# Sliding-window attention with ALiBi, then a hard-swish MoE layer: another PSUM bank plan for the end of batch 0

## The chip, the core and the metric
The kernel runs on one core of a Trainium2 chip. The metric is device time in microseconds (us), lower is better. The core's engines have queues of their own that run side by side and meet only at semaphores: TensorE (PE: matmuls, transposes as matmuls with an identity, and its weight loads, PEld), VectorE (DVE), ScalarE (ACT), GpSimd (POOL, which here also issues DMAs), and SyncE (SP, which only issues DMAs). Matmul results land in PSUM, which has eight banks[...].

## What is computed
For 8 batches of 8 heads, 576 positions and head size 64, attention looks back at most 127 positions and has a bias that falls with the distance; its output, 4608 tokens of 512 values, goes through two dense layers with a hard-swish between them.

```python
scores = scale * np.matmul(q, k.transpose(0, 1, 3, 2))
bias = slopes[:, None, None] * (-np.abs(rel).astype(np.float32))[None, :, :]
mask = (rel >= 0) & (rel < window)          # window = 128
scores = np.where(mask, scores + bias[None], -1000000000.0)
attn = softmax over the last axis
x = (attn @ v).transpose(0, 2, 1, 3).reshape(B * S, H * D)
h = x @ w_in                                # 512 -> 2048
out = (h * np.clip(h + 3.0, 0.0, 6.0) / 6.0) @ w_out
```

## The kernel before
**Pairs.** Attention is worked in 32 steps g, one for each pair of heads of a batch (NP = 4 pairs a batch: g 0 to 3 are batch 0, 4 to 7 batch 1). The steps of a pair are functions, each of which puts its instructions at the end of every engine's queue; the order is written out by hand (`tc.manual_schedule`), so the order of the calls is the order of each queue.

- `transposes(g)` (L218): 24 PE transposes of 96x64 make q and k column-wise, into two PSUM tiles `tp`. `settle(g)` (L237) copies them to SBUF (`qTb`, `kTb`).
- `scores(g)` (L248): matmuls into two double-bank tiles, `scd` (blocks on the diagonal) and `sco` (blocks beside it). For g up to 8 the bias comes in by a matmul with a table (L257, L260).
- `exp_diag`, `exp_off` (L285, L300): ACT takes exps of them to SBUF (`pd`, `po`, `p4buf`), POOL masks `po` (L306). In `first_batch` the three calls of a pair are `exps(g)`.
- `values(g, qts)` (L321): matmuls with v for query blocks 0 to 2 (tile `av`) and 3 to 4 (tile `avh`), each followed on DVE by the norm: a reciprocal (L343) and a multiplication into `avs` (L344). `both(g)` is the two calls.
- `back(g)` (L353): for batches 0 to 2, five PE transposes of `avs` into a tile `tb` (L364), and a copy of it into `xT` (L366), the input of the dense layers.

**Dense layers.** `moe_up` (L372) is a unit of four matmuls into a tile `hps` (L377), a relu on ACT (`r`, L381) and a product on DVE (`g`, L382) that frees the bank. `moe_down` (L385) is four matmuls of the second layer (L409). `fill(n)` (L429) puts the next n units into the queues. A unit of `moe_up` over 512 tokens needs all four pairs of their batch in `xT`.

**PSUM.** Four pools share the eight banks: `ps_sc` (two tiles of two banks, for scores), `ps_av` (one bank), `ps_h` (two banks) and `ps_o` (one bank). A tile waits until the last reader of the one that had its place before is done. In batches 0 and 1 `ps_h` holds `tp` and `hps`, `avh` is in `ps_h` for g below 3 and else in `ps_o`, and `tb` is in `ps_o`.

**Order.** `first_batch` (L504) runs pairs 0 to 3 up to their exps, with the transposes of the next pair in between; the values of pairs 0 to 3, their transposes back and pairs 4 and 5 of batch 1 follow in one stretch (the drain, L531 to L553). Then `segment` (L558) goes from g = 5 on: scores(g), transposes and settle of g+1, exps(g), values(g-1), back(g-1), with `fill` calls in between, whose numbers for g = 5 to 8 are in `FILLS` (L555). Loads stand in `stage_next(g)` (L443): POOL issues those of q and k of batches 0 to 2 (L101) and the weights (L169, L174), SP those of v and of later batches (L120). Values v are cast to bf16 by `cast_v` (L178). `more_constants` (L162) makes the eight biases `bias_d`, used from g = 9 on, and a memset of `tbuf`.

```python
        scores(3); exps(3); prepare(5); both(0); turn(4); both(1); stage_next(3)
        scores(4); exps(4); prepare(6); back(0); both(2); back(1)
        turn(5); both(3); back(2); stage_next(4)
        for j in range(3):
            cast_v(1, j, nc.gpsimd)
        scores(5); back(3)
```
(The drain, with its calls run together; `turn(g)` is transposes(g) and settle(g).)

Of the kernel before, what the change touches and what calls it, by code (L numbers as in the profile page):

```python
# [11 lines left out]
BF16 = mybir.dt.bfloat16  # L12
# [6 lines left out]
def kernel(  # L19
# [9 lines left out]
    nc = tc.nc  # L29
# [6 lines left out]
    NP = H // 2  # L36
# [4 lines left out]
    RP, RT = 96, 6  # L41
# [31 lines left out]
    ps_h = ctx.enter_context(tc.tile_pool(name="ps_h", bufs=2, space=bass.MemoryType.PSUM))  # L73
    ps_o = ctx.enter_context(tc.tile_pool(name="ps_o", bufs=1, space=bass.MemoryType.PSUM))
# [87 lines left out]
    def more_constants():  # L162
        for h in range(H):
            nc.vector.tensor_scalar(out=bias_d[:, h:h + 1], in0=rel_f, scalar1=-64.0,
                                    scalar2=slopes[h], op0=ALU.add, op1=ALU.mult)
        nc.gpsimd.memset(tbuf[64:128, :, 4, :], 0.0)
# [11 lines left out]
    def cast_v(b, j, eng):  # L178
        n = min(128, S - j * 128)
        copy = nc.scalar.copy if eng is nc.scalar else eng.tensor_copy  # L180
        copy(out=vbuf[b % 2][:n, j, :, 0:D], in_=ld[b, "v"][:n, j, :, :])
# [23 lines left out]
    def prepare(g):  # L205
        b, hp = divmod(g, NP)
        hs = slice(2 * hp, 2 * hp + 2)
        for nm in "qk":
# [6 lines left out]
            copy(out=pr, in_=wide[nm])  # L215
            st[g, nm] = pr

    def transposes(g):  # L218
        b, hp = divmod(g, NP)
        if g > 2 * NP:  # L220
            pair = ps_sc.tile([128, 2, 512], FP32, tag="sc", name="tpp")
        tps = {}
        for nm in "qk":
            src = st.pop((g, nm))
            if g > 2 * NP:
                tp = pair[:, "qk".index(nm), 0:S // 2].bitcast(BF16).rearrange(
                    "p (t a) -> p t a", t=RT)
            else:
                tp = ps_h.tile([128, RT, RP], BF16, tag="h", name="tp", padded_shape=[128, 8, 128])
            for t in range(RT):  # L230
                for e in range(2):
                    nc.tensor.transpose(tp[e * D:(e + 1) * D, t, :], src[:, e, ts(t, D)],
                                        ident[:RP, :RP])
            tps[nm] = tp
        st[g, "tps"] = tps

    def settle(g):  # L237
        b, hp = divmod(g, NP)
        tps = st.pop((g, "tps"))
        for nm, dst in (("q", qTb[b % 2]), ("k", kTb[b % 2])):  # L240
            eng = nc.scalar.copy if nm == "k" and g == 0 else nc.vector.tensor_copy
            eng(out=dst[:, hp, :, :].rearrange("p j c -> p (j c)")[:, 0:S].rearrange(  # L242
                "p (a t) -> p a t", t=RT), in_=tps[nm].rearrange("p t a -> p a t"))

# [76 lines left out]
    def values(g, qts):  # L321
        b, hp = divmod(g, NP)
        vb = vbuf[b % 2]
        pd, po, p4 = st[g, "pd"], st[g, "po"], p4buf[g % 4]
        if g < 2 * NP and qts[0] > 0:
            pool, tag = (ps_h, "h") if g < NP - 1 else (ps_o, "o")
            av = pool.tile([128, 3, 2, W], FP32, tag=tag, name="avh", padded_shape=[128, 3, 2, 85])
        else:
            av = ps_av.tile([128, 3, 2, W], FP32, tag="av", name="av")
        nq = len(qts)  # L330
        for i, qt in enumerate(qts):
            for e in range(2):
                h = 2 * hp + e
                if qt > 0:
                    nc.tensor.matmul(av[:, i, e, :], lhsT=po[:, e, qt - 1, :],  # L335
                                     rhs=vb[:, qt - 1, h, :], start=True, stop=False)
                d = pd[:, e, qt, :] if qt < 4 else p4[:, e, :]
                nc.tensor.matmul(av[:, i, e, :], lhsT=d, rhs=vb[:, qt, h, :],  # L338
                                 start=(qt == 0), stop=True)
        if qts[0] == 0:  # L340
            st[g, "avs"] = small.tile([128, NQ, 2, D], BF16, tag="avs", name="avs")
        rc = small.tile([128, 3, 2, 1], FP32, tag="rc", name="rc")
        nc.vector.reciprocal(rc[:, 0:nq, :, :], av[:, 0:nq, :, D:W])  # L343
        nc.vector.tensor_tensor(  # L344
            out=st[g, "avs"][:, qts[0]:qts[0] + nq, :, :], in0=av[:, 0:nq, :, 0:D],
            in1=rc[:, 0:nq, :, :].to_broadcast([128, nq, 2, D]), op=ALU.mult)
# [3 lines left out]
    def by_xbar(g):  # L350
        return XBAR_X and g >= NB_PE * NP and g % NP < NP - 1

    def back(g):  # L353
        b, hp = divmod(g, NP)
        avs = st[g, "avs"].rearrange("p j e d -> p j (e d)")
        if by_xbar(g):
            nc.sync.dma_start_transpose(
                out=xT[:, hp, ds(b * S, SP)].rearrange("p (j c) -> p j c", j=NQ),
                in_=avs.rearrange("p j c -> p (j c)"))
            return  # L360
        pool, tag = (ps_o, "o") if b < 2 else (ps_h, "h")
        tp = pool.tile([128, SP], BF16, tag=tag, name="tb", padded_shape=[128, 1024])
        for j in range(NQ):
            nc.tensor.transpose(tp[:, ts(j, 128)], avs[:, j, :], ident)  # L364
        eng = nc.scalar.copy if b == 0 and g != 2 else nc.vector.tensor_copy
        eng(out=xT[:, hp, ds(b * S, S)], in_=tp[:, 0:S])  # L366

    gts, ops = {}, {}
# [134 lines left out]

    def first_batch():  # L504
        transposes(0)
        settle(0)
        biases()
        prepare(1)
        def exps(g):
            exp_diag(g, 0)  # L510
            exp_off(g, 0)
            exp_off(g, 1)

        def both(g):
            values(g, (0, 1, 2))
            values(g, (3, 4))

        def turn(g):
            transposes(g)
            settle(g)  # L520

        for g in range(3):
            scores(g)
            exps(g)
            turn(g + 1)
            prepare(g + 2)
            for j, eng in (((0, nc.vector), (1, nc.vector)), ((2, nc.gpsimd),),
                           ((3, nc.vector), (4, nc.vector)))[g]:
                cast_v(0, j, eng)
            stage_next(g)  # L530
        more_constants()  # L531
        scores(3)
        exps(3)
        prepare(5)
        both(0)
        turn(4)
        both(1)
        stage_next(3)
        scores(4)
        exps(4)  # L540
        prepare(6)
        back(0)
        both(2)
        back(1)
        turn(5)
        both(3)
        back(2)
        stage_next(4)
        for j in range(3):
            cast_v(1, j, nc.gpsimd)  # L550
        scores(5)
        back(3)
        done[0] = NP  # L553

    FILLS = {5: (2, 0, 0, 0, 2, 2, 0), 6: (0, 0, 0, 0, 2, 2, 0),  # L555
             7: (0, 0, 0, 0, 2, 1, 0), 8: (0, 0, 0, 0, 2, 1, 0)}

    def segment(lo, hi, fills):  # L558
        for g in range(lo, hi + 1):
            f = fills(g)  # L560
            if by_xbar(g - 2):
                done[0] = g - 1
            pe_next = g + 1 < hi and (g + 1) // NP < NB_PE
            if lo < g < hi:
                scores(g)
            fill(f[0])
            if pe_next and g < 2 * NP:
                transposes(g + 1)
                settle(g + 1)
            if g == NP + 1:  # L570
                cast_v(1, 3, nc.vector)
                cast_v(1, 4, nc.vector)
            if g < hi:
                exp_diag(g, 0)
            fill(f[1])
            if g < hi:
                exp_diag(g, 1)
            if g >= lo:
                values(g - 1, (0, 1, 2))
            fill(f[2])  # L580
            if pe_next and g >= 2 * NP:
                transposes(g + 1)
            if g < hi:
                exp_off(g, 0)
            fill(f[3])
            if g < hi:
                exp_off(g, 1)
            if g >= lo:
                values(g - 1, (3, 4))
            if pe_next and g >= 2 * NP:  # L590
                settle(g + 1)
            fill(f[4])
            if g >= lo:
                back(g - 1)
                if not by_xbar(g - 1):
                    done[0] = g
            if g + 2 < hi and (g + 2) // NP < NB_PE:
                prepare(g + 2)
            fill(f[5])
            if g < hi:  # L600
                stage_next(g)
            fill(f[6])
# [3 lines left out]
    with tc.manual_schedule(engines=every):  # L606
# [11 lines left out]
        first_batch()  # L618
        segment(NP + 1, G, lambda g: FILLS.get(g, (1, 1, 1, 1, 1, 1, 2)))
        done[0] = G  # L620
# [34 lines left out]
```

## Time and profile before

| what | value |
|---|---|
| time, median of 5 runs | 342.98 us (342.53 to 345.0) |
| the profiled execution | 348.89 us, span 347.2 us |
| mean granted PE clock in it | 0.966 |
| busy: PE / DVE / ACT / POOL | 324.3 / 176.0 / 196.2 / 139.7 us |
| matmuls of the dense layers: L377 x576, L409 x560 | 150.8 us, 141.8 us |
| transposes back on ACT / DVE, first 70 us (copy xT, L366) | 638 / 450 ns |
| copies of q and k (L242) on ACT / DVE | 638 / 747 to 757 ns |
| DMA, first 80 us | 189 GB/s |

The page gives busy times of one profiled execution; the difference of 1.7 us between its time and its span lies outside the program's instructions. A row of the timeline is: start, duration (of a merged run), engine and line, operation, out<-in, and in square brackets how long the engine was idle before it and what released it. Granted clock is the share of full speed that PE was allowed.

### The profile page before, as it was taken

Reading aid. Unit: us, or ns where it says so; the run is one execution under the profiler, and the core shown is the slowest. Engines: PE = TensorE matmul, PEld = TensorE weight load, DVE = VectorE, ACT = ScalarE, POOL = GpSimd, SP = SyncE. Lnnn points to the kernel's source line nnn. Section 1 sums busy time; section 2 is a strip of 40 time slices with the busy share of each in tenths; the row PEclk is TensorE's granted clock in tenths of the full one; section 3 lists DMA queues with packets and bytes.
Section 4 is the critical chain, followed back from the end, with each engine's and each line's share of the span. In section 5 each row is a group of like instructions: output and inputs, shape, how many; then the busy total and the mean of one; then the engine's idle time right before and its main releaser. Section 6 shows DMA issues by size and latency. Waiting matters only on the chain.

```text
span 347.2 us, 7083 instructions
## 1 busy us (share of the span) xinstructions
PE 324.3 (93%) x2759; PEld 168.9 (49%) x2759; DVE 176.0 (51%) x364; ACT 196.2 (57%) x345; POOL 139.7 (40%) x246
## 2 busy tenths in 40 slices
PE   6777799899999999999999999999999999999995
PEld 5565355545444454444445545454554444444443
DVE  4664558766545554545455555545455534434410
ACT  3742457566666666666666666675766344343401
POOL 8645326736385465186456634733333000000000
PEclk9965679999999999999999999999999999999999
DMA  9999999999996899789949994520211000110021
GB/s 171 210 214 192 175 186 151 214 183 205 243 231 143 188 227 209 139 175 216 234 115 213 188 229 115 124 79 3 79 52 51 30 30 32 50 40 32 30 91 61
DMA packets 134865, 48.17 MB, mean 139 GB/s; under 512 B 121392, under 2 KB 130352, under 8 KB 134832
## 3 DMA queue, kind: packets, MB, share of 16 engines
q1 hardware_dynamic: 122464, 33.89, 53.4%
q0 software_dynamic: 8704, 7.44, 14.0%
q10 hardware_dynamic: 3664, 6.39, 5.3%
q8 instruction: 21, 0.34, 0.4%
q14 instruction: 12, 0.10, 0.1%
HBM read 36.70 MB, written 9.44 MB: 133 GB/s over the span
## 4 chain that ended last, share of the span: by engine, by line
PE 71%; ACT 7%; DVE 7%; issue 5%; DMA 4%; POOL 4%; SPq 2%; POOLq 0%; DVEq 0%
PE hps L377 31%; PE ops L409 27%; DVE g L382 3%; ACT r L381 3%; ACT po L303 2%; DMA ldbuf<-in_k_dram 2%; POOL pd L296 2%; SPq L120 2%; PE av L338 2%; PE scd L269 2%; DMA ldbuf<-in_q_dram 1%; PE sco L275 1%; PE av L335 1%; PE ops L393 1%; DVE qTb L242 1%
## 5 line engine op out<-in xcount | busy, mean ns | idle before, releaser
L382 DVE SCALAR_TENSOR_TENSOR g<-r,hps 128x512 bf16<-128x512 f32 x144 | 98.8, 687 | 137.1 <-ACT r L381 136.9
L381 ACT ACTIVATE r<-hps,bias 128x512 f32<-128x512 f32 x144 | 99.5, 691 | 112.1 <-PE hps L377 110.8
L377 PE MATMUL hps<-xT,w_in_sb 128*128 128x512 bf16 x576 | 150.8, 387 | 5.5 <-DVE g L382 5.5
L409 PE MATMUL ops<-w_out_sb,g 128*128 128x512 bf16 x560 | 141.8, 379 | 0.0
L409 PEld LDWEIGHTS <-g 128*128 128x128 bf16 x560 | 54.3, 98 | 63.6
L377 PEld LDWEIGHTS <-w_in_sb 128*128 128x128 bf16 x576 | 51.8, 99 | 60.8 <-issue 12.8
L306 POOL TENSOR_SCALAR_AFFINE_SELECT po<-po 128x512 bf16<-128x512 bf16 x62 | 39.1, 639 | 43.9 <-ACT po L303 41.1
L296 POOL TENSOR_SCALAR_AFFINE_SELECT pd<-pd 128x512 bf16<-128x512 bf16 x46 | 28.0, 632 | 46.7 <-ACT pd L293 46.5
L303 ACT ACTIVATE po<-sco,bias_o 128x512 bf16<-128x512 f32 x62 | 41.7, 687 | 0.0
L195 POOL CAST tbuf<-ldbuf 128x512 bf16<-128x512 f32 (+1 forms) x50 | 28.3, 611 | 29.9 <-issue 25.9
L344 DVE TENSOR_TENSOR avs<-av,rc 128x384 bf16<-128x384 f32 (+1 forms) x56 | 28.0, 500 | 1.9
L293 ACT ACTIVATE pd<-scd,bias_d 128x512 bf16<-128x512 f32 x46 | 28.9, 683 | 0.0
L338 PEld LDWEIGHTS <-pd 128*128 128x128 bf16 x248 | 18.9, 101 | 9.0
L335 PE MATMUL av<-vbuf,po 128*128 128x65 bf16 x220 | 21.3, 196 | 0.7 <-POOL po L306 0.7
L335 PEld LDWEIGHTS <-po 128*128 128x128 bf16 x248 | 19.4, 101 | 5.3 <-issue 1.5
L338 PE MATMUL av<-vbuf,pd 128*128 128x65 bf16 x234 | 21.7, 198 | 0.0
L415 ACT COPY osb<-ops 128x512 f32<-128x512 f32 x18 | 10.5, 586 | 12.8 <-PE ops L409 12.8
L314 ACT ACTIVATE p4buf<-sco,bias_d 128x64 bf16<-128x64 f32 x46 | 14.8, 322 | 0.0
L417 DVE COPY osb<-ops 128x512 f32<-128x512 f32 x17 | 11.6, 684 | 5.8 <-PE ops L409 5.8
L269 PE MATMUL scd<-qTb,kTb 64*128 64x128 bf16 x256 | 13.1, 225 | 0.0
L343 DVE RECIPROCAL rc<-av 128x6 f32<-128x6 f32 (+1 forms) x56 | 10.2, 182 | 3.9 <-PE av L338 3.9
L275 PE MATMUL sco<-qTb,kTb 64*128 64x128 bf16 (+1 forms) x256 | 12.2, 218 | 0.0
(85 smaller groups left out, 213.0 us busy)
## 6 DMA issues: line engine op xcount, KB each, us to landing
ldbuf<-in_v_dram SPq DMA_DIRECT2D x32, 256.0 KB, 5.6
out_dram<-osb ACTq DMA_DIRECT2D x23, 256.0 KB, 3.5
ldbuf<-in_q_dram SPq DMA_DIRECT2D x20, 256.0 KB, 5.2
ldbuf<-in_k_dram SPq DMA_DIRECT2D x20, 256.0 KB, 5.8
out_dram<-osb SPq DMA_DIRECT2D x12, 256.0 KB, 2.0
w_in_sb<-in_moe_w_in_dram POOLq DMA_DIRECT2D x4, 512.0 KB, 8.9
w_out_sb<-in_moe_w_out_dram POOLq DMA_DIRECT2D x4, 512.0 KB, 9.0
ldbuf<-in_v_dram SPq DMA_DIRECT2D x8, 128.0 KB, 6.2
```

Source lines behind the costliest of these rows:

```text
L195: nc.gpsimd.tensor_copy(out=tbuf[:m, :, j, :], in_=s[:m, j, :, :].rearrange("p (i e) d -> p i (e d)", e=2))
L293: nc.scalar.activation(out=pd[:, e, :, :].rearrange("p j c -> p (j c)"), in_=sc[:, e, :], func=ACT.Exp, bias=bias_d[:, h:h + 1], scale=scale)
L296: nc.gpsimd.affine_select(out=pd[:, e, :, :], in_=pd[:, e, :, :], pattern=[[0, 4], [1, 128]], channel_multiplier=-1, base=0, compare_op=AL ...
L303: nc.scalar.activation(out=po[:, e, :, :].rearrange("p j c -> p (j c)"), in_=sc[:, e, :], func=ACT.Exp, bias=bias_o[:, h:h + 1], scale=scale)
L306: nc.gpsimd.affine_select(out=po[:, e, :, :], in_=po[:, e, :, :], pattern=[[0, 4], [-1, 128]], channel_multiplier=1, base=-1, compare_op=A ...
L335: nc.tensor.matmul(av[:, i, e, :], lhsT=po[:, e, qt - 1, :], rhs=vb[:, qt - 1, h, :], start=True, stop=False)
L338: nc.tensor.matmul(av[:, i, e, :], lhsT=d, rhs=vb[:, qt, h, :], start=(qt == 0), stop=True)
L344: nc.vector.tensor_tensor(out=st[g, "avs"][:, qts[0]:qts[0] + nq, :, :], in0=av[:, 0:nq, :, 0:D], in1=rc[:, 0:nq, :, :].to_broadcast([128, ...
L377: nc.tensor.matmul(hps, lhsT=w_in_sb[:, ks, ts(ms, 128)], rhs=xT[:, ks, ts(nt, NT)], start=(ks == 0), stop=(ks == n_ks - 1))
L381: nc.scalar.activation(out=r6, in_=hps, func=ACT.Relu, bias=bias3[:, 0:1], scale=1.0 / 6.0)
L382: nc.vector.scalar_tensor_tensor(out=gts[nt][:, ms, :], in0=r6, scalar=1.0, in1=hps, op0=ALU.min, op1=ALU.mult)
L409: nc.tensor.matmul(ops[nt, sub], lhsT=gts[nt][:, ms, ts(sub, 128)], rhs=w_out_sb[:, ms, :], start=(ms == 0), stop=(ms == n_ms - 1))
```

## The change
The change touches batch 0 and the beginning of batch 1 only.

- Banks: `avh` is in `ps_o` except for g = 3; `tb` is in `ps_h` for g = 0, 1 and 3, and else, in batches 0 and 1, in `ps_o`; pair 5's `tp` are in a score tile (as those of g over 8 already are); k's `tp` of pairs 6 to 8 is in `ps_o`.
- Engines: ACT copies k of pair 4 and q and k of pair 5; of the copies of xT, ACT has pairs 0 and 3, DVE 1 and 2. Cast v(0,3) goes from DVE to POOL and stands a pair earlier; v(0,4) stays on DVE.
- Order: back(0) stands ahead of scores(4), back(1) right behind it, back(3) ahead of scores(5). `more_constants` goes from ahead of scores(3) to behind the casts of batch 1 in g = 5. The first two units of the dense layers in g = 5 stand apart, one ahead of pair 6's transposes, one behind them and exp_diag(5).

```diff
+    def in_sc(g):
+        return g > 2 * NP or g == NP + 1
+
     def transposes(g):
         b, hp = divmod(g, NP)
-        if g > 2 * NP:
+        if in_sc(g):
             pair = ps_sc.tile([128, 2, 512], FP32, tag="sc", name="tpp")
...
-            if g > 2 * NP:
+            if in_sc(g):
...
-                tp = ps_h.tile([128, RT, RP], BF16, tag="h", name="tp", padded_shape=[128, 8, 128])
+                pool, tag = (ps_o, "o") if nm == "k" and NP + 1 < g <= 2 * NP else (ps_h, "h")
+                tp = pool.tile([128, RT, RP], BF16, tag=tag, name="tp", padded_shape=[128, 8, 128])
...
-            eng = nc.scalar.copy if nm == "k" and g == 0 else nc.vector.tensor_copy
+            by_act = g == NP + 1 or (nm == "k" and g in (0, NP))
+            eng = nc.scalar.copy if by_act else nc.vector.tensor_copy
...
-            pool, tag = (ps_h, "h") if g < NP - 1 else (ps_o, "o")
+            pool, tag = (ps_h, "h") if g == NP - 1 else (ps_o, "o")
             av = pool.tile([128, 3, 2, W], FP32, tag=tag, name="avh", padded_shape=[128, 3, 2, 85])
...
-        pool, tag = (ps_o, "o") if b < 2 else (ps_h, "h")
+        pool, tag = (ps_h, "h") if b > 1 or g in (0, 1, 3) else (ps_o, "o")
...
-        eng = nc.scalar.copy if b == 0 and g != 2 else nc.vector.tensor_copy
+        eng = nc.scalar.copy if g in (0, 3) else nc.vector.tensor_copy
...
-            for j, eng in (((0, nc.vector), (1, nc.vector)), ((2, nc.gpsimd),),
-                           ((3, nc.vector), (4, nc.vector)))[g]:
+            for j, eng in (((0, nc.vector), (1, nc.vector)),
+                           ((2, nc.gpsimd), (3, nc.gpsimd)), ((4, nc.vector),))[g]:
                 cast_v(0, j, eng)
             stage_next(g)
-        more_constants()
         scores(3)
...
         both(1)
+        back(0)
         stage_next(3)
         scores(4)
         exps(4)
         prepare(6)
-        back(0)
+        back(1)
         both(2)
-        back(1)
         turn(5)
...
+        back(3)
         scores(5)
-        back(3)
         done[0] = NP

-    FILLS = {5: (2, 0, 0, 0, 2, 2, 0), 6: (0, 0, 0, 0, 2, 2, 0),
+    FILLS = {5: (1, 1, 0, 0, 2, 2, 0), 6: (0, 0, 0, 0, 2, 2, 0),
...
                 cast_v(1, 4, nc.vector)
+                more_constants()
```

## The prediction
> **What bounds the kernel now.** I read the slices of the page first, then TensorE's waits, then the timeline and the one-microsecond windows of the drain of batch 0.
>
> ```profile
> PE   6777799899999999999999999999999999999995
> PEclk9965679999999999999999999999999999999999
> DMA  9999999999996899789949994520211000110021
> ```
> A slice is 8.7 us. From the sixth on PE is full but for one, and from the seventh at full clock; the slack lies in the first 50 us, where PE stops and runs at half clock (slices 3 to 6). What PE waits for from 50 us to the end:
> ```profile
> PE hps L377 <- DVE g L382: 5.5, 12, 0.7
> PE av L335 <- POOL po L306: 0.7, 2, 0.3
> ```
> That is 6.2 us in 297 (1.1 in two more rows), in a pattern that repeats. So the end moves by what the start moves. My marker is the end of the sixth up-projection unit (four hps matmuls), 48.72 us (chain of waits: 46.19 + 2.53); after it the instruction order of every engine is the same in both kernels. Before it, the timeline has these PE stops:
> ```profile
> 21.02 0.69 PE L232 MATMUL tp<-ident,ldbuf 96*64 96x96 bf16 x12 [1.50 <-DMA ldbuf<-in_k_dram]
> ...
> 26.69 0.66 ACT L366 COPY xT<-tb 128x576 bf16<-128x576 bf16 x1
> 27.40 0.69 PE L364 MATMUL tb<-ident,avs 128*128 128x128 bf16 x5 [1.02 <-ACT xT L366]
> 28.82 0.76 DVE L242 COPY qTb<-tp 128x576 bf16<-128x576 bf16 x1 [1.52 <-PE tp L232]
> 29.50 0.75 DVE L242 COPY kTb<-tp 128x576 bf16<-128x576 bf16 x1
> 31.54 0.71 PE L364 MATMUL tb<-ident,avs 128*128 128x128 bf16 x5 [1.25 <-DVE avs L344]
> 39.40 0.45 PE L232 MATMUL tp<-ident,ldbuf 96*64 96x96 bf16 x12 [0.92 <-DVE g L382]
> 41.15 0.21 PE L338 MATMUL avh<-vbuf,pd 128*128 128x65 bf16 x1 [0.87 <-DVE vbuf L181]
> 41.92 0.21 PE L338 MATMUL avh<-vbuf,p4buf 128*128 128x65 bf16 x1 [0.39 <-DVE vbuf L181]
> ```
> Each number in brackets is idle PE. W0 (1.50) is a load. W1 (1.02): tb(1) wants the one ps_o bank, and ACT's copy of tb(0) stands behind the exps of pair 4. W2 (1.25): tb(2) wants ps_o again, which holds avh(3); its norm stands on DVE behind the two copies of pair 5. W3 (0.92): k's transposes of pair 6 want a ps_h bank that hps still holds. W4 (1.26): avh(4) wants batch 1's last values, cast behind all that on DVE. The clock in the same stretch:
> ```profile
> 20.00:21.00 1.00, 0.00 (x0) 0.00 (x0) 1.00 (x2) 0.68 (x2) 0.94 (x2) 0.68 1.22 196
> 30.00:31.00 1.00, 0.29 (x6) 0.13 (x3) 0.96 (x4) 0.00 (x0) 1.00 (x2) 0.50 1.24 206
> 38.00:39.00 1.00, 0.45 (x12) 0.32 (x12) 0.34 (x1) 1.00 (x2) 0.00 (x0) 1.00 1.25 216
> 43.00:44.00 1.00, 1.00 (x4) 0.34 (x3) 0.11 (x1) 0.01 (x1) 1.00 (x2) 0.50 1.03 153
> ```
> The first column is PE busy, the third from the end the granted clock: half from 20.35 to 37.4 and from 40.8 to 47.7.
>
> **How the profile stands to the median.** This execution took 348.89 us (span 347.2), 5.9 over the median of 342.98. I reckon the old start at full clock too, with the same durations for DVE and ACT and halved ones for PE: W1 and W2 grow (about 2.0 each, PE gets there sooner), W3 is 1.1, W4 1.6, and the marker falls at about 41.4, 7.3 earlier. 348.89 - 7.3 = 341.6, so the median run has some 1.4 us of half clock left. Both frames are used below.
>
> **The change, part by part.**
> Free edits, with their cover. Cast v(0,3): 0.62 us from DVE to POOL (rows: 0.63 there); its load is down by 15.0, POOL is idle from 16.30 to 16.98, and the select behind it feeds values of pair 2 after 24. bias_d and the tbuf memset leave 18.5; POOL's 0.69 goes into its 9.13 us wait for po (31.1 to 40.2); DVE's 0.56 goes between the casts of batch 1 and g(1): this one is not free and is counted below. kTb(4) on ACT (row: 0.64, DVE 0.75) at 21.75: ACT is idle from 20.7 to 24.5. avh(0) in ps_o spares k's transposes of pair 4 the wait for a norm that ends at 20.39, but the load of W0 lands at 20.97: zero. On SP, ACT and POOL the DMAs keep their order and the selects they stand behind, so W0 stays; w_in(1), behind the selects of pair 4, goes out up to 0.7 later than 27.3, lands at about 34.6 and is wanted by hps4, at 36.6 at the earliest. If these covers failed, together under 1 us.
>
> tb(0) now stands ahead of scores(4) on PE, 0.66 at half clock (0.35 at full), and delays scd(4), exps(4) and all behind them by as much. ACT copies xT(0) in that gap (0.64; idle until then). Then the sum at this profile's clock, PE rows in order: k transposes end 21.71; values(1) 1.1 -> 22.8; tb(0) 0.66 -> 23.5; scores(4) 0.85+0.11+0.17+0.43+0.37 = 1.93 -> 25.4; tb(1) (avs ready at 23.7, a free ps_h bank, no W1) -> 26.1; values(2) 1.0 -> 27.1; tpp(5) needs the bank of scd(4), read by ACT from 25.1 to 26.1: no wait, 1.17 -> 28.2; values(3) -> 29.2; tb(2) (ps_o free after norm(2), 28.0) -> 29.9; tb(3) waits for norm(3) (28.95 + 1.35 = 30.3), then -> 31.0; W2's 1.25 has become 0.4. scores(5) needs kTb(5): ACT ends p4 at 27.5, then two copies of at most 0.75 -> 29.0: no wait, -> 32.95. hps0 1.7 -> 34.65 (old: two units 34.83 to 37.91). tp(6) with k in ps_o, no W3, -> 35.85; hps1 waits for g0 (0.69 + 0.69 after 34.7) 0.3 -> 37.75 at the risen clock; casts on DVE are now ahead of g1: 38.25 and 39.1, so avh(4) ends at 39.3 (old 42.2). hps2 -> 40.2; hps3 waits for g1, late by bias_d's 0.56, 0.15 -> 41.6; tb(4) -> 42.4, hps4 -> 44.1, hps5 -> 45.8. Against 48.72: 2.9 us.
>
> The same at full clock: k transposes 21.4, values(1) 22.0, tb(0) 22.3, scores(4) 23.4, tb(1) 23.7, values(2) 24.25, tpp(5) 24.95 (scd(4) is read until 24.2, no slack), values(3) 25.55, tb(2) 25.9, wait for norm(3) 1.1, tb(3) 27.3, scores(5) 28.4 (kTb(5) at 26.9: 0.4 slack), hps0 29.3, tp(6) 30.0, wait g0 0.7, hps1 31.6, casts 32.7 and 33.3, avh(4) 33.5, hps2 34.4, hps3 35.5, norm(4) 35.9, tb(4) 36.2, hps4 after g2 37.5, hps5 38.4. Against 41.4: 3.0 us. Four waits of 7.0 (2.0+2.0+1.1+1.6 and 0.3) have become 4.0 (1.1+0.7+1.2 and three short ones).
>
> What the trace does not show is a copy of score-bank transposes on ACT into the stepped order. Nearest rows: ACT's kTb copy 0.64, DVE's tpp copies 0.75. I take 0.65; at 0.75 the slack of 0.4 still holds, so its bounds are 0 to 0.2 us.
>
> **The clock, row against rule.** The row: the clock fell at 20.35 and 40.8 though no PE wait was over 1.5 us; the 3.41 us before each fall were 54% and 53% busy (by the one-microsecond windows), and it rose only after 34.0 to 37.4 and 44.2 to 47.7, both full; stretches of 77 to 84% between did not bring it back, and one of 70% before did not lose it. The Trainium skill ("TensorE: Matmul & The Clock Gate", Part 1 and the closing table) says half rate comes after an idle window of some 3.4 us, so gaps under 3 us should be harmless. By the rule, removing waits of 1 to 2 us changes no clock: 3.0 us and no more. By the row, the new PE line, nearly full from 21.0 to 29.9, could bring the clock back at about 27: hps5 then ends near 41.2, 7.5 before this profile's marker. The row decides, but the median run has only 1.4 us of it to win; I take 0.3.
>
> So 342.98 - 3.0 - 0.3 = 339.7.
>
> **Rivals.**
> 1. Loads take the lead back. DMA is saturated up to 40 us. Pair 6's k lands at 29.02 and is wanted at 29.65 (full clock); w_in(2), issued behind the selects of pair 5, took 7.2 us here, 10.8 at worst, and would be issued at 34.2 and wanted at about 43.3. Against: 5 us of slack in the profile, and issue moves with the rest. Price 1 to 2.5: 341 to 342.2.
> 2. Slower: half clock under the new dense part. Place: 25.9 to 33.5 still holds waits of 1.1, 0.7 and 1.2. If a window there is some half busy, like the two above, the clock falls where hps units now run back to back, and each 3.41 us window of full PE costs 1.7. From three more windows than in the old kernel it decides: 5.1 - 3.0 = 2.1 slower, 345.1. Against: the new line is 75 to 85% busy there.
> 3. The waits only change owner: in the drain ACT gains three copies (kTb(4), qTb(5), kTb(5)) and loses xT(1), 1.3 us net in front of r0. If exps(4) come 1 us later than reckoned, tpp(5), kTb(5) and scores(5) follow, and two of three microseconds are gone: 342.0.
>
> **Chances.** Forecast 0.62 (338.3 to 341.2); rival 1 0.18; rival 3 0.10; rival 2 0.10. Faster by over 0.5% (under 341.27; less cannot be told from no change here) 0.70, within 0.5% 0.19, slower (over 344.7) 0.11. Range 337.8 (all half clock gone too: 342.98 - 3.0 - 1.4 = 338.6, and up to 0.8 of error in the waits) to 342.6, which takes in rivals 1 and 3.
>
> **What would show it.** Right: no wait of tb on ACT's xT, or on a norm over 1.2 us; k's transposes of pair 6 without a wait for g; the sixth hps unit ending 3 us earlier at equal clock; the same 6 to 7 us of PE waits after 50 us. Wrong: tp or hps waiting for a DMA between 28 and 50; scores(5) waiting for ACT's kTb; half clock beyond 38 us; or the earlier marker without an earlier end.

## The result and the profile after

| | before | after |
|---|---|---|
| time in the same measurement, median | 344.89 us (79 runs) | 345.53 us (44 runs) |
| ratio, 95% interval | | 1.0018 (1.0001 to 1.0035) |
| profiled execution, span | 348.89, 347.2 us | 345.62, 343.9 us |
| busy PE / DVE / ACT / POOL | 324.3 / 176.0 / 196.2 / 139.7 us | 318.6 / 172.8 / 197.2 / 139.8 us |

Forecast was 0.990 of before; measured is no change (at most 0.35% slower by the interval). The time goes with the granted clock: in some 150 runs of before that stand beside the experiments the median is 345.3 us at a mean clock of 0.98 and 343.7 at 0.99, and a straight line through all 182 falls by 1.5 us for each hundredth. The profiled run of before was one of the colder ones (0.966), that of after a usual one (0.988), so their difference of 3.3 us is not the change's.

The slices of the page of after, in the rows shown of before (8.6 us each):
```profile
PE   6678888979989999989999999999999999999995
PEclk9989999998999999999999999999999999999999
DMA  9999999999995999599949996510111000100021
```
Slices 3 to 6 were the cold ones of before, with PE busy for 7 to 9 tenths; now the clock is back after 3.4 us. In their place the ninth slice (7) and the twelfth (8) have idle PE, and the tenth a second dip of the clock. The DMA row is at 9 for the first twelve slices in both kernels and does not tell them apart; its bytes do: 4.03 MB between 42 and 65 us before, 4.47 after. PE's timeline of after (start, duration, [idle before, releaser]) answers the rows of the prediction:
```profile
27.35 0.34 PE L369 MATMUL tb<-ident,avs 128*128 128x128 bf16 x3 [0.36 <-DVE avs L349]
27.89 0.28 PE L369 MATMUL tb<-ident,avs 128*128 128x128 bf16 x2 [0.20 <-DVE avs L349]
...
31.69 1.02 PE L382 MATMUL hps<-xT,w_in_sb 128*128 128x512 bf16 x4 [0.87 <-DVE g L387]
...
41.43 0.19 PE L340 MATMUL avh<-vbuf,po 128*128 128x65 bf16 x1 [0.85 <-DVE kTb L247]
...
49.02 0.19 PE L340 MATMUL avh<-vbuf,po 128*128 128x65 bf16 x1 [0.85 <-DVE kTb L247]
```
(Line numbers are four or five higher behind the inserted function.) W1 is gone, W2 is down to 0.36 and 0.20, k's transposes of pair 6 do not wait, scores(5) does not wait for ACT's copy. The marker, the end of the sixth up-projection unit, is at 38.49 us; the full-clock column of the prediction said 38.4. The last two rows are new and were not foreseen: `avh` waits until DVE has copied k of a later pair out of the one `ps_o` bank. What PE waits for from 50 us on:
```profile
PE hps L382 <- DVE g L387: 4.8, 11, 0.7
PE tpp L236 <- ACT pd L298: 2.1, 1, 2.1
PE av L340 <- POOL po L311: 1.1, 3, 0.4
PE av L340 <- DVE avs L349: 0.7, 1, 0.7
```
The pattern of before is there, and beside it one wait of 2.1 us, for exps on ACT, and smaller ones for masks (POOL) and norms (DVE).

**Where the lead goes.** I set the ends of all 144 up-projection units of the two profiles side by side. After is 10.21 us ahead at the marker (this much because before had 23.9 us of half clock up to its marker, after 3.4), 8.72 at units 11 to 22, 5.03 at unit 23, 5.34 at unit 30, 4.2 from unit 32 on, 3.75 from unit 54, 3.2 from unit 86 to the last. The steps, in after's time, are at 41 to 50 us (1.5, the two new rows), at 73 to 79 (3.7), at 95 to 101 (1.1), at 145 to 149 and at 214 to 216 (0.5 each, masks that stand behind POOL's casts). Around the second step the timelines of POOL, ACT and PE of after say, in this order:
```profile
57.84 1.17 POOL L195 CAST tbuf<-ldbuf 128x512 bf16<-128x512 f32 x2
65.76 0.61 POOL L195 CAST tbuf<-ldbuf 128x512 bf16<-128x512 f32 x1 [6.75 <-DMA ldbuf<-in_q_dram]
68.10 0.61 POOL L195 CAST tbuf<-ldbuf 64x512 bf16<-64x512 f32 x1 [1.73 <-DMA ldbuf<-in_q_dram]
68.67 1.21 POOL L301 TENSOR_SCALAR_AFFINE_SELECT pd<-pd 128x512 bf16<-128x512 bf16 x2
```
```profile
72.73 0.37 ACTq L424 DMA_DIRECT2D out_dram<-osb  x1
73.20 0.69 ACT L386 ACTIVATE r<-hps,bias 128x512 f32<-128x512 f32 x1 [3.14 <-PE hps L382]
73.79 1.26 ACT L298 ACTIVATE pd<-scd,bias_d 128x512 bf16<-128x512 f32 x2
```
```profile
75.10 0.70 PE L236 MATMUL tpp<-ident,ldbuf 96*64 96x96 bf16 x24 [2.10 <-ACT pd L298]
```
POOL casts batch 3's q (loaded by SP) when it lands, and the masks of pair 9 stand behind that cast although their exps ended at 62.9. ACT's first output store (the ACTq row) stands from 70.06, when its data are ready, to 72.69: the trace has it waiting for the completion semaphore on which SP's last load of batch 3's k also counts, and that load landed at 72.66. The row of r names hps as releaser, but the hps was long done; the issue ahead of it held the queue. exps(10) stand behind the store, and PE behind exps(10); the clock falls for one window at 76.2. In before the same store goes out as soon as its data are there, 3.0 us after that load had landed (75.77):
```profile
78.20 0.58 ACT L415 COPY osb<-ops 128x512 f32<-128x512 f32 x1 [0.18 <-PE ops L409]
78.81 0.44 ACTq L419 DMA_DIRECT2D out_dram<-osb  x1
```
The third step is of the same kind. ACT's third store counts on one semaphore with a load of batch 4's k, which lands at 94.37 in after:
```profile
94.45 0.34 ACTq L424 DMA_DIRECT2D out_dram<-osb  x1
94.89 0.69 ACT L386 ACTIVATE r<-hps,bias 128x512 f32<-128x512 f32 x1 [2.36 <-PE av L343]
```
Its data were ready at 92.53. In before that load lands at 97.84 and the data are ready at 97.87: no wait, but no room either.

Those loads are late, as I read it, because POOL issues its own earlier. The first down-projection weights went out at 53.77 us before and at 43.55 after. In before POOL had no load under way from 36.23 to 41.54; in after this gap is 0.04 us long. So SP's loads of q, issued at 34 to 42 us before and 36 to 48 after, now run beside POOL's: they took 3 to 8 us each before and 10 to 24 after, and the last landed at 68.05 in place of 49.55. The first of k went out 9 us earlier than before; the last landed only 3 us earlier. The DMA view of 42 to 65 us of after (queue: packets, MB, share of 16 engines):
```profile
q0 software_dynamic: 3829, 3.46, 90.6%
q1 hardware_dynamic: 3828, 0.96, 31.8%
```
q0 is POOL's queue, q1 that of SP and ACT. They moved the same number of packets to within one (3,909 and 3,804 in e10 below). POOL's packets are 904 bytes on average, SP's 251, so SP gets 22% of the bytes, 42 GB/s, in this stretch. The Trainium skill ("DMA: Bandwidth & Descriptors", Queues, rings and completion order) says that a DMA engine goes round its queues a whole packet at a time, a packet being typically some 9 to 17 descriptors. What the profile counts as packets is smaller: SP's are the single rows of 256 bytes (64 values) that its loads are made of. That the turns of the two queues come out even in such pieces is what the counts here show, not what the page states. No run held POOL's loads back to see SP's speed up.

### The profile page after: what moved, and what is told of

It reads as the page before. It is cut to its first block, busy times and chain, and to the rows that moved or that the text cites. A ratio compares the mean times of both kernels' runs of the same rounds, so it can differ in the third digit from the quotient of the medians.

```text
span 343.9 us, 7081 instructions
## 1 busy us (share of the span) xinstructions
PE 318.6 (93%) x2759; PEld 164.8 (48%) x2759; DVE 172.8 (50%) x361; ACT 197.2 (57%) x347; POOL 139.8 (41%) x247
## 4 chain that ended last, share of the span: by engine, by line
PE 62%; DMA 13%; ACT 6%; issue 6%; DVE 5%; POOL 4%; SPq 3%; ACTq 0%; POOLq 0%
PE hps L382 27%; PE ops L414 27%; DMA ldbuf<-in_q_dram 8%; DMA ldbuf<-in_k_dram 5%; SPq L120 2%; ACT r L386 2%; DVE g L387 2%; POOL pd L301 2%; PE av L343 2%; ACT po L308 1%; PE av L340 1%; PE scd L274 1%; POOL tbuf L195 1%; ACT pd L298 1%; PE sco L280 1%
## 5 line engine op out<-in xcount | busy, mean ns | idle before, releaser
L382 PE MATMUL hps<-xT,w_in_sb 128*128 128x512 bf16 x576 | 148.0, 381 | 6.1 <-DVE g L387 6.0
L382 PEld LDWEIGHTS <-w_in_sb 128*128 128x128 bf16 x576 | 50.9, 98 | 59.3 <-issue 9.9
L340 PEld LDWEIGHTS <-po 128*128 128x128 bf16 x248 | 18.6, 99 | 6.0 <-POOL po L311 1.4
L188 POOL CAST vbuf<-ldbuf 128x1024 bf16<-128x1024 f32 x12 | 12.1, 1043 | 0.0
```

The source lines that it names most:

```text
L340: nc.tensor.matmul(av[:, i, e, :], lhsT=po[:, e, qt - 1, :], rhs=vb[:, qt - 1, h, :], start=True, stop=False)
L382: nc.tensor.matmul(hps, lhsT=w_in_sb[:, ks, ts(ms, 128)], rhs=xT[:, ks, ts(nt, NT)], start=(ks == 0), stop=(ks == n_ks - 1))
```

## The experiments

**Theory 1**: the start gains as reckoned, and late loads of batch 3 take it back through in-order queues. **Theory 2**: the lead was an artefact of a cold profile of before. A meeting, below, is an instruction in one of those queues that has to wait for such a load. In the expectations, "rival 3" is that the two waits above are the whole loss (not the prediction's third).

**Before again**, unchanged.

> The kernel before, unchanged, for a second profile and the null ratio (0.998 to 1.002 by both theories). Theory 1 (the new plan does win 3 us in batch 0, and loses them at 73 to 80 us to two waits that hang on batch 3's q and k loads): its sixth hps unit ends near 41.4 us if the clock stays full (48.7 if it falls as in the first profile), ACT's first output store waits for less than 1 us, and at equal clock the marker is 3 us behind the kernel after. Theory 2 (no lead was there: the first profile of before was an unusually cold run, and a typical one is as early as the kernel after): the sixth hps unit ends at 38.5 to 39.5 us, and the same stall of about 3 us stands at 73 to 80.

0.9977 (0.9939 to 1.0015), as it should be. In the profile (clock 0.978) the marker is at 46.81: neither the full-clock start nor as cold as the first. There is no stall at 73 to 80, ACT's store waits for nothing, and from the marker to the last unit it takes 279.3 us, as in the first profile of before. After takes 286.3. Theory 2 asked for a marker of 38.5 to 39.5 and a stall; both are absent. Half clock still makes up 13.7 us of its start.

**Batch 3's q and k not loaded**, in after and in before; the kernel leaves out these loads, and the attention of batch 3 works on older values.
```diff
     def load_tokens(b, nm):
...
         ld[b, nm] = t
+        if b == 3 and nm in "qk":
+            return
```

> The kernel after without the loads of batch 3's q and k; its attention then works on the older values in those slots, so that part of the computation is left out. Theory 1: the wait of POOL's cast and of ACT's first store go, the idle stretch of PE at 73 to 80 us and the half clock behind it go too, and 3 to 4 us come off: 0.987 to 0.992 of before (about 340.5 where before is 343 to 345). Theory 2: the same as e5 within 0.3%, both 0.99 to 1.0 of before.

> The same loads (batch 3's q and k) left out of the kernel before; that part of the computation is left out in the same way. Theory 1: before does not hang on these loads, so 0.997 to 1.001 of before, and e4 is 3 us (0.9%) faster than this. Theory 2: as much is gained here as in e4, so the two agree within 0.3%.

After: 0.9783 (0.9732 to 0.9834), 338.48 us. Before: 0.9962 (0.9930 to 0.9994), 344.44 us. Theory 2 wanted them equal; they are 1.8% apart. Theory 1 was off in size: the loads cost the kernel after twice what it had said, and before gains 0.4% where it had said 0.3% at most. In the profile of e4 no PE wait is left behind 50 us but the old ones.

**The two waits moved out of the way**: together (e6), and each alone (e2, e3).
```diff
-        if g == 8:
-            cast_tokens(3, "q")
         if g == 9:
             load_tokens(3, "v")
+            cast_tokens(3, "q")
             xbar(3, "q")
+        if g == 10:
             cast_tokens(3, "k")
-        if g == 10:
             xbar(3, "k")
```
```diff
-            eng = nc.sync if done[0] == G else nc.scalar
+            eng = nc.sync if done[0] == G else nc.gpsimd if (nt, sub) == (0, 0) else nc.scalar
```
(The first is e2, the second e3, both together e6; `xbar` is the transposing DMA from `tbuf`.)

> The kernel after with both waits moved out of the way: POOL's casts of batch 3's q and k stand a step later, behind the masks, and the first output store is issued by POOL and not by ACT. All loads and all work stay. Theory 1: ACT and POOL no longer stand idle for loads at 65 to 73 us, PE no longer waits 2 us for pd at 75, and it takes 0.988 to 0.993 of before, near e4. Theory 2: as the kernel after, 1.000 to 1.003.

> The kernel after with only the casts of batch 3's q and k a step later on POOL (behind the masks of that step); the first store stays on ACT. Theory 1, as it stands after e4 to e6: every in-order queue that meets a late load passes the lateness on, so removing one such meeting moves the stall to the next one. POOL's 6.8 us of waiting for q at 59 to 66 us goes, ACT's store still waits for the last k load, and the end moves by less than 1.5 us: 0.997 to 1.004 of before. Rival 3 (these two waits are all of the loss): a third to a half of e4's gain, 0.987 to 0.992.

> The kernel after with only the first output store moved from ACT to POOL. Theory 1: ACT's 3.1 us wait at 70 to 73 us goes and the stall of PE at 75 with it, but the time lands on a later meeting with a load (POOL's cast behind the transposing DMA of batch 4's q at 100 to 106, as in e6): 0.997 to 1.004 of before. Rival 3: 3 us come off for good, 0.990 to 0.993.

e6: 1.0009 (0.9983 to 1.0034). Theory 1 in its first form, with these two waits as the loss, had wanted 0.988 to 0.993, and falls. Theory 2 had wanted 1.000 to 1.003, but e1 and the pair e4 and e5 speak against it. The profile shows what became of the gain: at 103.5 us e6 is still 5.9 us ahead of after, and at 113.5, two units on, it is level. POOL's and PE's timelines of e6:
```profile
106.02 2.84 POOL L195 CAST tbuf<-ldbuf 128x512 bf16<-128x512 f32 x5 [9.27 <-DMA qTb<-tbuf]
108.81 1.22 POOL L301 TENSOR_SCALAR_AFFINE_SELECT pd<-pd 128x512 bf16<-128x512 bf16 x2
```
```profile
109.50 0.20 PE L343 MATMUL av<-vbuf,pd 128*128 128x65 bf16 x1 [2.75 <-POOL pd L301]
```
The cast of batch 4's k into `tbuf` waits 9.3 us for the transposing DMA of q out of the same buffer, which SP issues only behind its late loads; the masks stand behind the cast again. e2 alone gave 1.0010 (0.9984 to 1.0036) with the same wait of 9.4 us at 98 to 107, so the first wait is not the loss. e3 alone gave 0.9975 (0.9946 to 1.0004): the stall at 75 is gone, and the next store of ACT waits 6 us, from 80 to 86, for the transposing DMA of k, with which it shares a semaphore; so the second is not the loss either. The form that is left: each in-order queue that meets a late load passes the lateness on, and taking one meeting away leads to the next.

**More meetings taken away**: e6, and from batch 4 on the cast of the next batch's k one step later (e8), its transposing DMA another step later (e10).
```diff
-            if hp < 2:
-                xbar(b + 1, "qk"[hp])
             if hp in (0, 2):
+                xbar(b + 1, "qkk"[hp])
+            if hp in (1, 2):
                 cast_tokens(b + 1, "kkv"[hp])
```
(This is e10; e8 keeps k's transposing DMA at hp = 1, behind the cast.)

> e6, and in batches 3 to 6 POOL's cast of the next batch's k stands a step later (just ahead of its transposing DMA), so that it no longer meets the transposing DMA of q that shares its buffer. Nothing is left out. Theory 1: the 9.3 us for which POOL waited at 97 to 106 us in e6 goes, the masks run on time, the lead of 5.9 us that e6 still had at 105 us is kept to the end, and it takes 0.978 to 0.985 of before. If the wall is the DMAs' bandwidth itself and not the queue order, another queue meets the loads and it stays at 0.995 to 1.003.

> e8 with the transposing DMA of k yet a step later on SP, so that SP does not wait for the cast in front of its loads. Theory 1: SP's waits for POOL's casts go, the loads behind them are issued up to 3 us earlier; as e8 within 0.3% if nothing else meets the loads, 0.2 to 0.5% better if SP's waiting mattered.

e8: 0.9849 (0.9808 to 0.9889), at the upper end of what was expected. e10: 0.9826 (0.9783 to 0.9868), 340.46 us; the two cannot be told apart by time. The loads, bytes and work are those of after, and between 42 and 65 us SP's queue moves 0.96 MB in e10 too, so it is the order of the queues and not the bandwidth as such. In e10 the cast of batch 4's k still waits, but with the masks of the pair ahead of it:
```profile
102.08 1.23 POOL L301 TENSOR_SCALAR_AFFINE_SELECT pd<-pd 128x512 bf16<-128x512 bf16 x2 [4.59 <-ACT pd L298]
...
108.57 2.84 POOL L195 CAST tbuf<-ldbuf 128x512 bf16<-128x512 f32 x5 [2.83 <-DMA qTb<-tbuf]
```

**The orders of e10 without the change (e11), and their last part alone (e14).**

> The kernel before with the queue orders of e10 (casts of batch 3's q and k a step later, first store on POOL, casts and transposing DMAs of k a step later from batch 4 on): e10 without the change under study. Theory 1: before starts late enough to miss most late loads, so it gains at most 1%: 0.990 to 0.999 of before, and e10 (0.983) is ahead of it by the change's own 3 us and the clock it wins, 0.8 to 1.6%. If the orders alone made e10's gain: 0.983 to 0.986.

> The kernel after with only the part of e10 from batch 4 on (cast and transposing DMA of the next batch's k a step later); batch 3's casts and the first store stay. Theory 1: the wait of ACT's store at 70 to 73 us and the 3 to 4 us behind it stay, but nothing is lost after that: 0.991 to 0.999 of before, between the kernel after and e10. If the first two meetings cost nothing in themselves, as e2 and e3 alone suggest: 0.982 to 0.986, as e10.

e11: 0.9958 (0.9931 to 0.9986). The orders alone are worth 0.4%; with the change 1.7%. So where PE waits for no load, the change itself takes 1.3% off, 4.6 us give or take 1.7. e14: 0.9976 (0.9943 to 1.0010), in its range, but its reason held only in part. It had said that nothing is lost behind the first stall; that stall is shorter here (PE waits 1.0 us), and PE is only 69% busy at 90 to 100 us. There ACT's third store stands, as in after, but for longer:
```profile
95.99 0.34 ACTq L424 DMA_DIRECT2D out_dram<-osb  x1
96.43 0.69 ACT L386 ACTIVATE r<-hps,bias 128x512 f32<-128x512 f32 x1 [4.74 <-DMA ldbuf<-in_k_dram]
```
The load that it shares a semaphore with landed at 95.92.

**A later start on purpose**: 50 idle matmuls of PE (2.96 us) ahead of the first up-projection unit, in after (e12) and in e10 (e13).
```diff
         first_batch()
+        spin(50)
```

> The kernel after with 50 idle matmuls of 128 columns on PE between scores(5) and the first up-projection unit: the start of everything behind is some 2.8 us later at full clock, nothing else changes. Theory 1: the end hangs on loads and not on this start, so the 2.8 us are swallowed by the waits behind and the end moves by less than 1 us: 1.000 to 1.005 of before. If the end follows the start: 1.008 to 1.011.

> The same 50 idle matmuls in e10, where no queue waits for a load any more. Theory 1: here the end follows the start, 2.3 to 2.9 us more than e10: 0.989 to 0.992 of before. If something other than the loads had absorbed the start in the kernel after, it would absorb it here too: 0.982 to 0.985.

e12: 0.9974 (0.9949 to 1.0000), under the 1.000 to 1.005 that theory 1 had said and far from 1.008; 3 us more at the start cost nothing at the end. Its first store stands for 0.6 us only, but its third holds ACT for 3.61 us, until the load of batch 4's k lands at 96.50. In after, e12, e14 and e16 (below) the marker moves by 3.8 us, and the last up-projection unit comes 229.1 to 230.4 us after that landing. e13: 0.9900 (0.9866 to 0.9933), 0.7% or 2.6 us more than e10, give or take 1.9, as expected. The end follows the start where the loads are out of the way.

**The two new waits** behind the drain: k's transposes of pairs 7 and 8 back in `ps_h`, in e10 (e15) and in after (e16).
```diff
-                pool, tag = (ps_o, "o") if nm == "k" and NP + 1 < g <= 2 * NP else (ps_h, "h")
+                pool, tag = (ps_o, "o") if nm == "k" and g == NP + 2 else (ps_h, "h")
```

> e10 with k's transposes of pairs 7 and 8 back in the bank pair of the up-projection, as before; pair 6's stay in the one-bank pool. Theory 1 with the two new waits (values of pairs 5 and 6 for VectorE's copy of k) as a real cost: both waits go, the lead between the sixth and the twelfth up-projection unit is kept, and 1.5 us come off e10: 0.976 to 0.981 of before. If those waits only stand in the place of waits that come anyway: as e10, 0.981 to 0.985.

> The same bank choice alone in the kernel after, with its queue orders untouched. Theory 1: the start of everything behind is 1.5 us earlier and the waits on loads swallow it: 0.999 to 1.004 of before. If the end follows the start: 0.996 to 0.998.

e15: 0.9788 (0.9734 to 0.9841), 339.08 us, the fastest version here that does all the work. By time alone it is not apart from e10; the profile is plain: its lead over e10 is 2.87 at the marker and 4.37 at the twelfth unit, in two steps of 0.75 where the two rows of 0.85 were, and PE has no wait of avh for kTb left. (The 2.87 go with the clock: e10's start has 6.8 us of half clock, e15's none.) The still earlier start meets loads again: PE waits 0.7 us for the weights of the down-projection and 1.2 for the transposed k. e16: 0.9985 (0.9956 to 1.0013), between the two ranges, so the time does not decide. In its profile the two waits are gone, and ACT's third store stands until 94.53, as in after (94.41), with 4.56 us of idle ACT in place of 2.36.

All profiles side by side, with the marker and the time from it to the end of the last up-projection unit:

| kernel | ratio | marker | marker to last unit |
|---|---|---|---|
| before, first / again | 1, 0.9977 | 48.70 / 46.81 | 279.3 / 279.3 |
| e5, e11 (plan of before) | 0.9962, 0.9958 | 44.68, 46.96 | 279.4, 278.3 |
| after | 1.0018 | 38.49 | 286.3 |
| e2, e3, e6 (one or two meetings away) | 1.0010, 0.9975, 1.0009 | 37.12, 38.91, 37.11 | 287.5, 286.6, 286.2 |
| e12, e14, e16 | 0.9974, 0.9976, 0.9985 | 42.29, 39.48, 40.53 | 284.2, 285.5, 283.8 |
| e4, e10, e13 | 0.9783, 0.9826, 0.9900 | 38.67, 39.95, 41.41 | 279.8, 279.8, 279.8 |
| e8 | 0.9849 | 40.11 | 280.9 |
| e15 | 0.9788 | 37.07 | 280.4 |

In the rows of after and its near relatives the marker moves by 5.2 us and the last unit stays between 323.3 and 326.5, with a lean of some 0.4 us for each of the marker's. In the others the last unit follows the marker.

## Why the prediction was wrong

- **The drain: right in its parts, lucky in its sum.** W1 and W3 are gone, W2 is 0.56 in two parts (put at 1.1 for full clock), and ACT's copies of pair 5 cost nothing; rival 3 (the waits change owner to ACT) did not happen. At full clock the marker was put at 38.4 and stood at 38.49, but that is not the sum that was made. One window of half clock is in it (21.54 to 24.96, PE full, so about 1.7 us). Against that PE got past its first wait for k at 20.23 and not at about 21.0, W2 was shorter (the wait for g0 longer, 0.87 in place of 0.7), and the wait for the casts, put at over 1, shrank to about 0.2 because PE came later. In e2, e6 and e15, whose starts have no half clock, the marker is at 37.07 to 37.12. What the plan is worth up to the marker at equal clock can only be estimated: with 0, 3.4 and 6.8 us of half clock the new plan has its marker at 37.1, 38.5 to 39.5 and 40.0 to 40.5, some 1.5 us later for each window; that line gives 41.7 at the 10.2 us of e5, which has the plan of before and stands at 44.68. This is the 3.0 that was forecast.
- **The clock, right in direction and too small.** It fell at 21.54 and at 76.2 though in the 3.41 us before PE had no gap over 1.3 and 2.1 us (55% and 38% busy), so the row was a better guide than the rule of 3 us; it came back at 24.96, after one full window. (Three small readings of the prediction are off and change no sum: it leaves out one stretch, 30.6 to 34.0, with 72%; PE busy is the second column of its windows; the 1.52 in brackets is idle DVE.) Rival 2 (half clock at 25.9 to 33.5) did not happen in this profile. But 0.3 us was set, from a median of 342.98 taken as nearly warm; over 79 runs it is 344.89. Over many runs before has a median clock of 0.979, after 0.989, e10 0.991; at the 1.5 us that goes with a hundredth in before's runs, that is 1.5 to 1.8 us.
- **The step that failed: "So the end moves by what the start moves", with its reason that behind the marker the order of every engine is the same in both kernels.** It failed twice. First, the order is the same but the banks are not: the change reaches past the beginning of batch 1, to k of pair 7 and of pair 8, the first of batch 2. Their transposes and `avh` of pairs 5 and 6 now share the one `ps_o` bank, and the values wait for DVE's copy. That costs 1.50 us (e15 against e10), so the plan was worth some 1.5 and not 3.0 at equal clock. Second, PE's waits of before said nothing of how much room the loads had: 3.0 us at ACT's first store and 0.03 at its third. POOL's loads moved ahead with the start, SP's landed later or hardly earlier, and the queues behind them met them late. From marker to last unit after takes 7.0 us more (286.3 against 279.3): 1.5 for the banks, 3.7 at the first store with the half clock behind it, 1.1 at the third, 1.0 at later masks, less 0.3 won back on the way.
- **Rival 1 had the kind and not the place.** It named pair 6's k and the third part of w_in, at 1 to 2.5 us; neither was waited for. It was put down with "issue moves with the rest": that held for POOL's queue and not for SP's. The loads were those of batches 3 and 4, and the price was all of the gain.
- The sum with these terms: -3.0 (estimated) + 1.5, and -1.5 to -1.8 of clock, is about -3.2; e10 beside e11 shows -4.6 (-2.8 to -6.3), an interval that holds both. The late loads give it back in the kernel after.

What stays open: that SP's loads are late because of POOL's is read from the traces, and no run held POOL's loads back. Why e12 comes out 0.4% under after was not tried (the intervals nearly touch; its median clock was 0.993 against 0.989, which would go with 0.2%).

## What to carry over

Where a change moves a start forward, list which transfers move with it and which are tied to something else, and look two or three stages ahead for in-order queues that will meet the ones left behind: a row of waits that is short in the old kernel shows no slack, only that nothing was late (a store of before had 0.03 us to spare). To find out whether an end follows a start, put a dead delay in: where it costs nothing, the start is not the bound. Where a PSUM plan is changed, go through every tile that shares the new bank, behind the stage in question too.

## Not expected of the hardware

- Two busy DMA queues shared the engines by packets and not by bytes: 3,829 against 3,828 packets in 23 us, 904 and 251 bytes each. The queue with the short rows fell behind the one with the long rows (24.0 us for a load of 256 KB, where 5.2 is the median of all such loads of q).
- A store on a compute engine's queue can hold that engine for the sake of another queue's load: ACT stood 2.6 us ahead of a 0.37 us issue, because both transfers count on one semaphore.
- The clock fell at 21.54 us in after with PE idle for 1.3 us at most in one piece in the 3.41 us before (55% busy); the windows before that one, 60% and 70% busy, had not lost it. It came back after one full window. In before it fell after a window of 54% and took from 20.35 to 37.4: four windows of 72 to 85% did not bring it back, a full one did.
